# A fused linear-attention and gated state-space kernel: copies, scans and transposes in another order, and a flag read earlier

## The chip, the cores and the metric

The kernel runs on one core of one Trainium2 chip. The metric is device time in microseconds (us) of one launch. The core has five engines that run their own instruction streams and meet at semaphores: TensorE (PE in the profile, its weight loads PEld), VectorE (DVE), ScalarE (ACT), GpSimd (POOL) and SyncE (SP), which here only issues DMAs. Matmul results land in PSUM banks; everything else lies in SBUF.

## The reference, cut to what matters

Two blocks follow one another. The first is a recurrence per batch and head, the second a gated scan between two matrix products:

```python
# q, k, v, alpha: (4, 8, 768, 48)
for t in range(S):
    state = alpha[:, :, t, :, None] * state + np.einsum('bhd,bhe->bhde', k[:, :, t], v[:, :, t])
    y[:, :, t] = np.einsum('bhd,bhde->bhe', q[:, :, t], state)
x = y.transpose(0, 2, 1, 3).reshape(B, S, H * D)          # (4, 768, 384)

proj = x @ w_in                                           # 384 -> 2 * 512
val, gate = proj[..., :D_inner], proj[..., D_inner:]
a = np.exp(A_log)
for t in range(S):
    h = a[0, 0] * h + val[:, t, :]
    ys[:, t, :] = h
silu = gate * (1.0 / (1.0 + np.exp(-gate)))
return silu * ys @ w_out                                  # 512 -> 384
```

## The kernel before

**Tiling.** The 4 x 768 steps are cut into 12 blocks of 256 steps, three to a batch. A block of the attention is worked in chunks of 64 steps: the decays are folded into the operands as running products (tile `P`, a scan forward over `al`, the turned alphas; tile `V`, a scan backward), so that inside a chunk everything is matmuls. Zq is q times `P`, Zk is k times `V`. Raw q, k and alpha come from DRAM in rows and are turned on VectorE with `turn` (line 600, one instruction of 128x1024 elements each).

**One turn.** The main loop runs over `n` from 0 to 11; its turns overlap three blocks. In turn `n` the kernel projects block `n` with `w_in` (four calls of `project`, 12 matmul records each on line 988, 48 in all), does values, states and the carried part of the attention of block `m = n + 1` (`second` and `third`: lines 834, 866, 847), and prepares block `n + 2`: its alphas were turned at the end of the turn before, its k and q are turned and scaled during the turn, its scores (line 798) and masks come at the end. `project(n, cc)` also has a scan `hh` on VectorE (line 995) that reads its PSUM bank, a Silu on ScalarE (`sg`, line 1006) and a product `f_last` on GpSimd (line 1008). Because only four PSUM banks are handed round for such products (the string `taken` fixes which), `project(n, 3)` writes the bank that the scan of `project(n, 1)` has read.

**Order by hand.** The schedule is manual: each engine runs its instructions as the Python program emits them, and only semaphores make it wait. The preparation of a block is a generator, `products(l)`, with a `yield` behind each step: turn alpha, turn k, scan P, scan V, Zk, turn q, Zq. `go(count)` advances it, so where `go` stands decides where these VectorE instructions lie among the scans `hh`.

**Output.** For turns 2 to 10 the product with `w_out` is done in seven half-size products instead of eight (`output_parts(n)`, line 1064 for the matmuls and 1072 for the PSUM copies on ScalarE). It is a generator too. `pa` is a product whose copy goes to `s1` (profile name `wide`), `pd` one whose copy goes to `s7` (profile name `wide_S`, the copy to a tile that no matmul reads), `pc` one whose copy goes to `s5` (`wr`). After its copy, the bank `pa` takes a second product on top, and so do `pd` (records `mm<-wide_S,f_last`) and `pc`. TensorE runs: `pa` (4 records), `pd` (4), `pc` (4), second `pa` (4), second `pd` (4), `pb` (4), second `pc` (4), 28 in all. The second product on a bank waits for the copy from it.

**y's way into xT.** `join(m, engines)` copies the two PSUM tiles of y to `yst` (lines 960, 961), moves pieces of it that change partitions by eight DMAs (line 963, four on SP, four on POOL), and returns `rest`, which copies the straight pieces, two of 48x256, directly from PSUM to `xT` on ScalarE (line 966).

**Turns that end differently.** Turns 1 and 3 (`late`) leave the scores and masks of the next block until behind their output products; turn 1 has a body of its own, turn 3 ends in the `else` branch, and so does turn 10, which has no further block to prepare. Turn 2 and turns 4 to 9 end in the branch with `masks(..., between=...)`: the first part of `output_parts` is emitted between the mask products, then `rest()`, then the next part.

**Flag.** The fast path checks that its inputs allow the folded decays. `check_flag` (end of turn 10) reduces the checks to one integer in SBUF, every engine reads it into a register (line 1342, at the end of turn 11) and branches at line 1366: to a general version, or to the last output product (line 1373). On the measured inputs the latter is taken.

Of the kernel before, what the change touches and what calls it, by code (L numbers as in the profile page):

```python
# [346 lines left out]
def fast(  # L347
# [22 lines left out]
    nc = tc.nc  # L370
# [6 lines left out]
    NG = S // GC  # L377
    N = B * NG
# [23 lines left out]
    def load_raw(name, m, engine):  # L402
        if m >= N:
            return
        b, g = divmod(m, NG)
        src = srcs[name]
        to = raws[name][:, 0:4 * ROW].rearrange("p (h x) -> p h x", h=4)
        for i in range(2):
            for odd in range(2):
                n = ROW - 16 - 16 * odd  # L410
                engine.dma_start(
                    out=to[ds(64 * i + 32 * odd, 32), :, 0:n],
                    in_=src[b, ds(4 * i, 4), ds(g * GC, GC), :]
                    .rearrange("h (c j) d -> c h (j d)", c=32)[:, :, ds(32 * odd, n)])
# [77 lines left out]
    flag = const.tile([1, 1], I32, name="flag")  # L492
# [194 lines left out]
    def bank(tag=None):  # L687
        if tag:
            return ps_at.tile([C, 512], FP32, tag=tag, name=tag)
        return ps_mm.tile([C, 512], FP32, tag=f"mm{next(taken)}", name="mm")  # L690
# [376 lines left out]
    def output_parts(n):  # L1067
        b, g = divmod(n, NG)
        (B11, B12), (B21, B22) = blocks
        T1, T2, T3 = sums_w  # L1070
        S1, S2, S3, S4, U2, s5 = (parts_f[x] for x in ("S1", "S2", "S3", "S4", "U2", "s5"))
        copy = lambda to, t: nc.scalar.activation(to, t, AF.Copy)
        pa, pd = [bank()[:, 0:HM] for _ in range(2)]
        product(pa, quarter(0, 0), B11, True)
        copy(s1, pa)
        product(pd, S3, T3, True)
        yield
        copy(s7, pd)
        pc = bank()[:, 0:HM]
        product(pc, S1, T1, True)  # L1080
        copy(s5, pc)
        product(pa, quarter(0, 1), B21, False)
        o_sb = [rows.tile([C, DM], FP32, tag="o_sb", name="o_sb") for _ in range(G)]
        copy(o_sb[0][:, 0:HM], pa)
        product(pd, quarter(1, 1), T4, False)
        pb = bank()[:, 0:HM]
        product(pb, S2, T2, True)
        product(pc, S4, B22, False)
        nc.gpsimd.tensor_add(s7, s7, s5)
        yield  # L1090
        nc.vector.tensor_add(U2, s1, pb)
        nc.vector.tensor_add(o_sb[1][:, 0:HM], U2, pd)
        nc.vector.tensor_add(o_sb[0][:, HM:], U2, pc)
        nc.gpsimd.tensor_add(o_sb[1][:, HM:], U2, s7)
        for c in range(G):
            nc.sync.dma_start(out=out[b, ds(g * GC + c * C, C), :], in_=o_sb[c])
        yield
# [28 lines left out]
    last = P[:, :, GC]  # L1126
# [63 lines left out]
    for n in range(N):  # L1190
# [37 lines left out]
        elif n == 1:  # L1228
            scores(m)
            masks(m)  # L1230
            h3, f3 = project(0, 3, True)
            f2()
            P = scan_P(3)
            h3()
            values(m, True)
            st = states(m)
            add_banks(m, st)
            for f in fs_late:
                f()
# [12 lines left out]
            load_v(4, nc.sync)  # L1252
            f1()
            junk(3)
            V = scan_V(3, P)
            f2 = project(n, 2)
            scaled_k(3, tk, V)
            f2()
            output(0)
            sum_weights()  # L1260
            f3 = project(n, 3)
            tq = plain("q")
            turn("q", tq)
            load_raw("q", 4, nc.sync)
            scaled_q(3, tq, P)
            f3()
            go(1)
        else:
            if n == 2:
                first(m)  # L1270
            if n - 1 not in late:
                go(1)
                if n == N - 2:
                    check_w(5)
                next(outs, None)
                second(m)
                go(1)
                if n == N - 2:
                    check_w(0)
            else:  # L1280
                go(2 if n == 2 else 1)
            f0 = project(n, 0)
            f0()
            if n == N - 2:
                check_w(1)
            if n == 2:
                go(1)
            load_raw("a", n + 3, nc.sync)
            load_raw("k", n + 3, nc.sync)
            go(1)  # L1290
            f1 = project(n, 1)
            f1()
            if n < N - 1:
                sum_early()
            if n - 1 in late:
                second(m)
            if n == 4:
                go(1)
            if n == N - 2:
                check_w(2)  # L1300
            go(1)
            f2 = project(n, 2)
            f2()
            if n == N - 2:
                check_end()
            go(1)
            load_raw("q", n + 3, nc.sync)
            f3 = project(n, 3)
            f3()
            if m + 1 < N:  # L1310
                go(1)
            if n == N - 3:
                check_w(3)
            if n < N - 1:
                sum_late()
            rest = third(m)
            if n < N - 1:
                outs = output_parts(n)
            if n not in late and m + 1 < N:
                scores(m + 1)  # L1320
                masks(m + 1, between=lambda: next(outs))
                if m >= NG:
                    rest()
                    add_up(m, (3,))
                next(outs)
                go(1)
                if n == N - 3:
                    check_w(4)
            else:
                if m < N and m >= NG:  # L1330
                    rest()
                    add_up(m, (3,))
                if n < N - 2:
                    go(1)
                    for _ in outs:
                        pass
            load_v(m + 2, nc.sync)
        if n == N - 2:
            check_flag()
        if n == N - 1:  # L1340
            tc.mark_branch_hint_location("last", hint=0, engines=[mybir.EngineType.PE, mybir.EngineType.Activation, mybir.EngineType.DVE, mybir.EngineType.SP, mybir.EngineType.Pool])
            value = nc.values_load(flag[0:1, 0:1], min_val=0, max_val=1)
        if n == 1:
            output(n)
        if n == N - 2:
# [66 lines left out]
```

## Time and profile before

| what | value |
|---|---|
| median of 3 runs | 273.99 us (273.46 to 274.56) |
| the profiled execution's own time | 274.39 us |
| span of the profile | 272.7 us, 9967 instructions |
| PE busy | 265.9 us, 97% of the span |
| DVE busy | 234.7 us, 86% |
| POOL busy | 161.6 us, 59% |
| ACT busy | 111.5 us, 41% |
| granted TensorE clock | 0.999 of full speed |

The profile is of one execution. A row of its timeline reads: start in us from the span's start, duration, engine, line of the kernel, operation, output<-inputs by the program's names, shapes, count of merged records, and in brackets the engine's idle time before it with what ended that time. Two things must be known to read it. A matmul record lasts longer than the distance to the next one, since matmuls are pipelined, so distances between starts say more than durations. And four records that begin on a waiting engine are listed with 0.92 us instead of 0.81, so a held group can be told by its duration.

### The profile page before, as it was taken

How to read it: one execution, taken by the hardware profiler on the slowest of the kernel's cores; microseconds unless marked ns; L12 is line 12 of the kernel's file. 1: busy time of each engine (PE TensorE's matmuls, PEld its weight loads, DVE VectorE, ACT ScalarE, POOL GpSimd, SP SyncE). 2: the span in 40 equal slices, each digit the busy share in tenths (PEclk: the TensorE clock that was granted, in tenths of full speed). 3: DMA queues.
4: the chain of work that ended last, by engine and by line, in shares of the span. 5: the costliest groups of instructions: out<-in, count | busy, mean ns of one | idle time of the engine just before them, and what ended most of it. 6: DMA issues, size and time to landing. Idle time of an engine off the chain costs nothing.

```text
span 272.7 us, 9967 instructions
## 1 busy us (share of the span) xinstructions
PE 265.9 (97%) x4168; PEld 230.3 (84%) x4168; DVE 234.7 (86%) x316; ACT 111.5 (41%) x270; POOL 161.6 (59%) x185
## 2 busy tenths in 40 slices
PE   8999999999998999999999999999999999999995
PEld 6988888877786888888988988988988889888874
DVE  6979998996899999699999998999998998882430
ACT  3767766462341631441542433524525515214111
POOL 8122323175116997689985995996876976646000
PEclk9999999999999999999999999999999999999999
DMA  6937984998692669396588479595587501201101
GB/s 185 308 123 239 295 188 154 241 194 208 195 219 72 139 158 226 94 232 160 113 213 174 103 193 196 118 242 143 138 206 158 139 2 31 75 0 46 60 7 58
DMA packets 52304, 41.19 MB, mean 151 GB/s; under 512 B 27392, under 2 KB 50944, under 8 KB 52256
## 3 DMA queue, kind: packets, MB, share of 16 engines
q1 hardware_dynamic: 49328, 37.34, 55.2%
q0 software_dynamic: 1536, 2.20, 3.0%
q10 hardware_dynamic: 1392, 0.99, 1.2%
q8 instruction: 34, 0.56, 0.9%
q14 instruction: 14, 0.11, 0.2%
HBM read 32.54 MB, written 4.72 MB: 137 GB/s over the span
## 4 chain that ended last, share of the span: by engine, by line
PE 82%; DVE 10%; issue 2%; ACT 2%; DMA 1%; POOL 1%; DVEq 0%; ACTq 0%; POOLq 0%
PE mm L988 42%; PE mm L1064 15%; PE y L834 4%; PE y L847 4%; PE mm L1022 4%; PE mm L798 3%; PE s L798 3%; PE s L866 3%; DVE P L635 2%; PE mm L1373 2%; DVE V L654 2%; PE mm L707 1%; DMA raw_a<-in_alpha_dram 1%; DVE hh L995 1%; DVE k L600 1%
## 5 line engine op out<-in xcount | busy, mean ns | idle before, releaser
L988 PE MATMUL mm<-xT,w_in 128*128 128x256 f32 x576 | 129.7, 382 | 0.8 <-DVE hh L995 0.7
L988 PEld LDWEIGHTS mm<-xT,w_in 128*128 128x128 f32 x576 | 107.8, 190 | 16.9 <-DVE hh L995 1.1
L1006 ACT ACTIVATE sg<-mm 128x256 f32<-128x256 f32 x48 | 18.4, 384 | 89.2 <-PE mm L988 84.2
L1008 POOL TENSOR_TENSOR f_last<-sg,hh 128x256 f32<-128x256 f32 x36 | 30.2, 845 | 30.6 <-ACT sg L1006 21.7
L886 POOL TENSOR_TENSOR sum<-sum,dS 128x192 f32<-128x192 f32 x30 | 38.3, 1276 | 3.7 <-ACT dS L874 2.3
L635 DVE TENSOR_TENSOR_SCAN P<-al,lower 128x1028 f32<-128x1028 f32 x12 | 30.1, 2510 | 0.3
L995 DVE TENSOR_TENSOR_SCAN hh<-a_dec,hh,mm 128x256 f32<-128x256 f32 x32 | 23.4, 730 | 8.0 <-PE mm L988 7.7
L654 DVE TENSOR_TENSOR_SCAN V<-al,ends 128x1028 f32<-128x1028 f32 x12 | 29.3, 2439 | 0.4
L963 POOL DMA_DIRECT2D xT<-yst x44 | 22.5, 516 | 4.6 <-ACT yst L960 3.2
L556 POOL TENSOR_TENSOR w_in<-w_in,wr 128x768 int32<-128x768 int32 x4 | 7.3, 1823 | 25.9 <-DVE wr L551 16.1
L1064 PE MATMUL mm<-wide,wr 128*128 128x192 f32 x108 | 20.5, 326 | 0.0
L600 DVE STREAM_TRANSPOSE k<-raw_k 128x1024 f32<-128x1024 f32 x9 | 18.4, 2049 | 0.0
L600 DVE STREAM_TRANSPOSE q<-raw_q 128x1024 f32<-128x1024 f32 x9 | 18.2, 2025 | 0.0
L1064 PEld LDWEIGHTS mm<-wide,wr 128*128 128x128 f32 x108 | 18.0, 190 | 0.0
L818 POOL TENSOR_TENSOR AK<-AK,mask 128x512 f32<-128x512 f32 x9 | 13.4, 1494 | 7.7 <-ACT AK L814 7.6
L874 ACT ACTIVATE dS<-s 128x384 f32<-128x384 f32 (+1 forms) x18 | 7.4, 461 | 23.8 <-PE s L866 23.8
L619 DVE TENSOR_TENSOR Zk<-k,V 128x1024 f32<-128x1024 f32 (+1 forms) x14 | 16.5, 1181 | 0.1
L600 DVE STREAM_TRANSPOSE al<-raw_a 128x1024 f32<-128x1024 f32 x8 | 16.4, 2051 | 0.0
L1064 PE MATMUL mm<-w_out,f_last 128*128 128x192 f32 x72 | 15.8, 342 | 0.1
L610 DVE TENSOR_TENSOR Zq<-q,P 128x1024 f32<-128x1024 f32 (+1 forms) x14 | 15.2, 1087 | 0.0
L847 PEld LDWEIGHTS y<-Zq,sum 48*64 48x64 f32 x656 | 11.7, 134 | 3.9 <-issue 2.5
L834 PEld LDWEIGHTS y<-AK,v 64*64 64x64 f32 x352 | 12.1, 134 | 2.9 <-issue 2.9
(188 smaller groups left out, 503.4 us busy)
## 6 DMA issues: line engine op xcount, KB each, us to landing
v<-in_v_dram SPq DMA_DIRECT2D x22, 192.0 KB, 3.3
out_dram<-o_sb SPq DMA_DIRECT2D x22, 192.0 KB, 2.7
raw_k<-in_k_dram SPq DMA_DIRECT2D x18, 184.0 KB, 4.7
raw_q<-in_q_dram SPq DMA_DIRECT2D x18, 184.0 KB, 4.3
raw_k<-in_k_dram SPq DMA_DIRECT2D x18, 176.0 KB, 5.0
raw_q<-in_q_dram SPq DMA_DIRECT2D x18, 176.0 KB, 4.7
wbits<-in_moe_w_in_dram SPq DMA_DIRECT2D x8, 384.0 KB, 5.4
raw_a<-in_alpha_dram SPq DMA_DIRECT2D x16, 184.0 KB, 3.9
```

Of the source, the lines that this page charges most:

```text
L600: nc.vector.transpose(out=by_runs(to).rearrange("p h c j -> p h j c"), in_=raws[name][:, 0:4 * ROW].rearrange("p (h j d) -> p h j d", h=4, ...
L635: nc.vector.tensor_tensor_scan(out=P, data0=al[:, 0:4 * GP], data1=lower.rearrange("p h t -> p (h t)"), initial=0.0, op0=ALU.mult, op1=ALU ...
L654: nc.vector.tensor_tensor_scan(out=V[:, ::-1], data0=al[:, 1:4 * GP + 1][:, ::-1], data1=ends.rearrange("p h t -> p (h t)")[:, ::-1], init ...
L834: nc.tensor.matmul(ys[m][i][ds(64 * s, 64), e, ds(c * C + h * L, L)], v_sb[rows, c, 4 * i + p, :], As[i][rows, c, p, :], start=across and ...
L847: nc.tensor.matmul(ys[m][i][ds(64 * s, 64), e, ds(u * L, L)], Ss[j][rows, p, :], Zqs[m % 2][rows, u, p, D:], start=False, stop=True, skip_ ...
L886: nc.gpsimd.tensor_add(Ss[j][:, :, 0:D], Ss[j - 1][:, :, 0:D], part)
L963: engines[n % len(engines)].dma_start(out=xT[to, a], in_=st[rows, i, e])
L988: nc.tensor.matmul((pv, pg)[vg], w_ins[cc][:, kk, vg, :], xT[:, kk, :], start=(kk == 0), stop=(kk == NK - 1))
L995: nc.vector.tensor_tensor_scan(out=hh, data0=a_dec[:, cc:cc + 1].to_broadcast([C, GC]), data1=pv, initial=prev_h[cc][:, GC - 1:GC] if n % ...
L1006: nc.scalar.activation(sg, pg, AF.Silu)
L1008: f = lambda: engine.tensor_mul(fs[n][cc], sg, hh)
L1064: nc.tensor.matmul(o, a[:, k], b[k] if type(b) is list else b[:, k], start=start and k == 0, stop=k == KC - 1, skip_group_check=True)
```

## The change

No instruction is added or taken away; all edits move instructions in the order of an engine.

1. In `output_parts`, a `yield` is added behind the copy of `s7`. At the ends of turns 2 and 4 to 9, `next(outs)` is called once more ahead of `rest()`, so that the copy `s7` goes ahead of y's two straight copies. At the ends of turns 3 and 10, `next(outs)` is called twice ahead of `rest()`, so that both copies, `s1` and `s7`, go ahead of them. In turn 10 the tiny matmul of `check_flag` (line 587) comes to stand behind the first 8 of the 28 records as a consequence.
2. In turn 2, the scan `hh` of `project(2, 1)` goes ahead of the product Zk of block 4 (one `go(1)` moves from ahead of `project(2, 1)` to behind `f1()`).
3. At the end of turn 1, block 4's k is turned right behind its alphas (`go(2)` for `go(1)`), ahead of the two mask products `A` of block 3 on VectorE, and turn 2 has one `go` fewer.
4. In turn 11, the flag is read into registers ahead of `project(11, 3)` instead of behind it.

```diff
@@ output_parts
         product(pd, S3, T3, True)
         yield
         copy(s7, pd)
+        yield
         pc = bank()[:, 0:HM]
         product(pc, S1, T1, True)
         copy(s5, pc)
@@ end of turn 1
             scaled_q(3, tq, P)
             f3()
-            go(1)
+            go(2)
@@ turns 2 and on
             else:
-                go(2 if n == 2 else 1)
+                go(1)
             f0 = project(n, 0)
...
             load_raw("k", n + 3, nc.sync)
-            go(1)
+            if n != 2:
+                go(1)
             f1 = project(n, 1)
             f1()
...
-            if n == 4:
+            if n in (2, 4):
                 go(1)
...
             load_raw("q", n + 3, nc.sync)
+            if n == N - 1:
+                tc.mark_branch_hint_location("last", hint=0, engines=[...])
+                value = nc.values_load(flag[0:1, 0:1], min_val=0, max_val=1)
             f3 = project(n, 3)
             f3()
...
                 masks(m + 1, between=lambda: next(outs))
-                if m >= NG:
-                    rest()
-                    add_up(m, (3,))
+                next(outs)
+                rest()
+                add_up(m, (3,))
                 next(outs)
                 go(1)
...
             else:
-                if m < N and m >= NG:
+                if m < N:
+                    next(outs)
+                    next(outs)
                     rest()
                     add_up(m, (3,))
...
-        if n == N - 1:
-            tc.mark_branch_hint_location("last", hint=0, engines=[...])
-            value = nc.values_load(flag[0:1, 0:1], min_val=0, max_val=1)
```

More of the change, by code (lines that the diff above doesn't have):

```diff
@@ L1307, in fast @@
             load_raw("q", n + 3, nc.sync)
+            if n == N - 1:
+                tc.mark_branch_hint_location("last", hint=0, engines=[mybir.EngineType.PE, mybir.EngineType.Activation, mybir.EngineType.DVE, mybir.EngineType.SP, mybir.EngineType.Pool])
+                value = nc.values_load(flag[0:1, 0:1], min_val=0, max_val=1)
             f3 = project(n, 3)
@@ L1339, in fast @@
             check_flag()
-        if n == N - 1:
-            tc.mark_branch_hint_location("last", hint=0, engines=[mybir.EngineType.PE, mybir.EngineType.Activation, mybir.EngineType.DVE, mybir.EngineType.SP, mybir.EngineType.Pool])
-            value = nc.values_load(flag[0:1, 0:1], min_val=0, max_val=1)
         if n == 1:
```

## The prediction

> **What bounds the kernel now.** I read the busy time by stretches first, then TensorE's own rows wherever one group starts later than its predecessor's pace would have it, then the engine that released it.
>
> ```profile
> 131.00:264.00 133.00, 132.56 (x1942) 117.91 (x1941) 114.85 (x149) 48.25 (x127) 92.38 (x105) 1.00 0.50 120
> ```
>
> The columns behind the length are PE, PEld, DVE, ACT and POOL. PE is busy 132.56 of 133.00 us, at full granted clock: half of the kernel is TensorE alone, and an edit on another engine is worth only what it takes out of PE's row of starts. Busy time hides small holds, because a record lasts longer than its distance to the next one. So I go by starts. References first, from the chain of waits and from turn 10:
>
> ```profile
> 122.07 5.38 PE mm L988 x24
> 148.22 0.47 PE y L847 x32
> ...
> 251.00 0.81 PE L1064 MATMUL mm<-wide_S,f_last 128*128 128x192 f32 x4
> 251.65 0.81 PE L1064 MATMUL mm<-wide,wr 128*128 128x192 f32 x4
> ```
>
> Unheld, 24 projection records take 5.38 us (2.69 for 12), 32 carried records 0.47, four output records 0.65 (251.65 - 251.00) with a listed duration of 0.81. Now PE in turn 2:
>
> ```profile
> 80.16 2.86 PE L988 MATMUL mm<-xT,w_in 128*128 128x256 f32 x12
> 83.67 2.86 PE L988 MATMUL mm<-xT,w_in 128*128 128x256 f32 x12 [0.65 <-DVE hh L995]
> 86.46 0.46 PE L847 MATMUL y<-Zq,sum 48*64 48x64 f32 x16
> 87.20 0.41 PE L847 MATMUL y<-Zq,sum 48*64 48x64 f32 x16
> 87.85 0.46 PE L847 MATMUL y<-Zq,sum 48*64 48x64 f32 x16 [0.23 <-POOL sum L886]
> 88.13 0.95 PE L798 MATMUL s<-Zq,Zk 48*64 48x112 f32 x32
> 91.83 0.81 PE L1064 MATMUL mm<-w_out,f_last 128*128 128x192 f32 x4
> 92.89 0.92 PE L1064 MATMUL mm<-wide_S,f_last 128*128 128x192 f32 x4 [0.24 <-ACT wide_S L1072]
> ```
>
> Three holds. The projections take 86.46 - 80.16 = 6.30 instead of 5.38: 0.92 lost on the scan `hh`. The last 32 carried records take 88.13 - 87.20 = 0.93 instead of 0.47: 0.46 lost on GpSimd's `sum`. The second `pd` comes 92.89 - 91.83 = 1.06 behind the second `pa` instead of 0.65, 0.41 late, and starts slowly, 0.92 instead of 0.81: 0.52 lost on the copy `s7`. Together 1.90.
>
> ```profile
> 109.25 1.46 PE L1064 MATMUL mm<-wide,wr 128*128 128x192 f32 x8
> 110.80 0.92 PE L1064 MATMUL mm<-w_out,f_last 128*128 128x192 f32 x4
> 131.23 1.46 PE L1064 MATMUL mm<-wide,wr 128*128 128x192 f32 x8
> 132.53 0.81 PE L1064 MATMUL mm<-w_out,f_last 128*128 128x192 f32 x4
> 133.25 0.92 PE L1064 MATMUL mm<-wide_S,f_last 128*128 128x192 f32 x4
> ...
> 232.35 0.92 PE L1064 MATMUL mm<-wide_S,f_last 128*128 128x192 f32 x4
> 248.81 1.46 PE L1064 MATMUL mm<-wide,wr 128*128 128x192 f32 x8
> 250.25 0.92 PE L1064 MATMUL mm<-w_out,f_last 128*128 128x192 f32 x4
> ```
>
> Eight records at pace take 132.53 - 131.23 = 1.30. In turn 3 the second `pa` starts 1.55 behind, 0.25 late, plus 0.11 of slow start: 0.36. In turn 10 it is 1.44, 0.14 late, plus 0.11: 0.25. In turns 4 to 9 (first at 133.25, last at 232.35, six) the second `pd` starts 0.72 behind the second `pa` instead of 0.65, plus 0.11: 0.18 each. No wait list shows these six; the 0.92 does. Nothing else behind 92 us is held, apart from the branch at the end. All holds that the change can reach: 1.90 + 0.36 + 6 x 0.18 + 0.25 = 3.59 us.
>
> **Edit 1, the copies.** What the second `pd` waits for, in turn 4:
>
> ```profile
> 132.08 0.76 ACT L966 ACTIVATE xT<-y 48x256 f32<-48x256 f32 x2
> 132.87 0.33 ACT L1072 ACTIVATE wide_S<-mm 128x192 f32<-128x192 f32 x1
> ```
>
> The copy ends at 133.20, PE starts at 133.25. With the order changed it takes the place at 132.08. Its own input, the first `pd`, is the first half of the group at 131.23, whose fourth record starts 3 x 0.16 later at 131.72; with the 0.33 that one record lasts (0.81 less three steps of 0.16) it is done at 132.05. So the copy ends near 132.41, 0.77 ahead of the 133.18 at which PE would come unheld. The hold goes: 6 x 0.18 = 1.08. The two straight copies move 0.33 back and end near 133.17; ahead of the next projection, which reads xT, PE still has the 12 records from 133.18 on, 3 x 0.65 = 1.95 us, and `s5`, next on ScalarE, keeps its place. No DMA and no queue is passed, and none is issued by the moved copies. Without that cover, a straight copy that came last would cost at most its own 0.33 a turn. Bounds: 0 to 1.08; I take 1.08.
>
> In turns 3 and 10 both `s1` and `s7` (0.33 each) pass the straight copies (0.76), so PE's second `pa`, 0.25 and 0.14 late, is covered: 0.36 and 0.25. In turn 10 xT is wanted at once, as turn 11 projects right behind the 28 records. The pieces moved by DMA are not touched. The first `pd` is done at 248.81 + 0.49 + 0.33 = 249.63, `s7` at 249.96, the straight copies 0.76 later at 250.7, and PE ends the 28 records at 251.65 + 2 x 0.65 - 0.25 = 252.7: 2 us to spare. I take 0.61 for both turns, and 0.5 as lower bound, since the flag's matmul now stands among the 28 and may start slowly once more (0.11).
>
> **Edits 2 and 3, VectorE in turn 2.** VectorE's rows, and GpSimd's beside them:
>
> ```profile
> 69.81 2.02 DVE L600 STREAM_TRANSPOSE al<-raw_a 128x1024 f32<-128x1024 f32 x1
> 72.79 0.42 DVE L813 TENSOR_TENSOR A<-s,mask 128x256 f32<-128x256 f32 x1 [0.96 <-PE s L798]
> 73.56 0.42 DVE L813 TENSOR_TENSOR A<-mm,mask 128x256 f32<-128x256 f32 x1 [0.34 <-PE mm L798]
> 73.90 2.05 DVE L600 STREAM_TRANSPOSE k<-raw_k 128x1024 f32<-128x1024 f32 x1
> 75.80 2.23 DVE L635 TENSOR_TENSOR_SCAN P<-al,lower 128x1028 f32<-128x1028 f32 x1
> 81.73 1.23 DVE L619 TENSOR_TENSOR Zk<-k,V 128x1024 f32<-128x1024 f32 x1
> 82.87 0.74 DVE L995 TENSOR_TENSOR_SCAN hh<-a_dec,hh,mm 128x256 f32<-128x256 f32 x1
> 85.99 1.35 DVE L610 TENSOR_TENSOR Zq<-q,P 128x1024 f32<-128x1024 f32 x1
> ...
> 74.22 1.28 POOL L818 TENSOR_TENSOR AK<-AK,mask 128x512 f32<-128x512 f32 x1 [5.75 <-ACT AK L814]
> 85.66 2.13 POOL L886 TENSOR_TENSOR sum<-sum,dS 128x192 f32<-128x192 f32 x2
> ```
>
> `hh` ahead of Zk saves it 82.87 - 81.73 = 1.14: it would end at 83.61 - 1.14 = 82.47, and PE wants the bank at 80.16 + 2.69 = 82.85. The 0.92 goes even if VectorE gains nothing else. Zk comes later by one scan, 0.7 us; the scores want it at 88.13, or at 86.75 if all comes.
>
> The k transpose would start behind al, at 71.7, and fill the 0.96 + 0.34 us in which VectorE waits for scores. Its rows of k were asked for early:
>
> ```profile
> 61.63 1.96 SPq L411 DMA_DIRECT2D raw_k<-in_k_dram  x4
> ...
> DMA to landing us min/median/max: 3.0/4.3/5.3
> ```
>
> Issued by 63.59, landed by 68.9 at the latest: 2.8 us to spare. The load of the next k goes out behind it and stays behind alpha's four DMAs on SP. Two transposes at 75.80 - 73.90 = 1.90 put the first `A` at 69.81 + 3.80 = 73.61 and, at 0.34 each, P at 74.29, 1.51 us earlier. The later `A` are no loss: the values that read them stand behind 24 projection records, at 73.5 + 5.38 = 78.9 or so, and the PSUM bank of the second `A` behind 12. But where P would start GpSimd's AK product runs, from 74.22 to 75.50. How these two meet is shown elsewhere:
>
> ```profile
> 93.21 3.27 DVE L635 TENSOR_TENSOR_SCAN P<-al,lower 128x1028 f32<-128x1028 f32 x1
> ...
> 116.08 3.18 POOL L818 TENSOR_TENSOR AK<-AK,mask 128x512 f32<-128x512 f32 x1 [1.86 <-ACT AK L814]
> ```
>
> P takes 2.23 alone but 3.27 where GpSimd was already at work; the AK product takes 1.28 alone but 3.18 where P had just begun. The one that starts second waits. [...]
>
> By the starts above AK leads by 0.07 us, so I take P as second: it ends at 75.50 + 2.23 = 77.73 instead of 78.03. VectorE's chain gains 0.30. Then the sums: GpSimd's second sum ends at 85.66 + 2.13 = 87.79, 0.45 behind the end of Zq at 87.34, since Zq held it. Zq's end moves to 87.04, the sum's to 87.49, and PE gains 0.30 there, not 0.92 + 0.46 = 1.38. The 0.52 of `s7` comes on top, because that copy, 0.41 late, now passes 0.76 us of copies. So turn 2 gives 0.82. If P is first, Zq ends at 85.83 and the sum at 86.28, ahead of PE, which would want it at 87.85 - 1.38 = 86.47, and all 1.90 comes. Bounds: 0.52, if VectorE gains nothing, to 1.90. In turn 3 PE would then be 0.4 us or so earlier than VectorE is; whether the scans there keep pace I leave to the third rival.
>
> **Edit 4, the flag.** Register loads and branches, by line, and the chain of waits at the end:
>
> ```profile
> L1342 PEldq TENSOR_LOAD <-flag x1: 486/486/486, 259.4 to 259.4; - x1
> ...
> L1366 PEldq COMPARE_BRANCH  x1: 3708/3708/3708, 260.0 to 260.0; - x1
> ...
> 263.47 0.44 issue
> ```
>
> PE's sequencer read the flag at 259.4, 4 us ahead of the array's last projection at 263.47; then the branch sat 3.71 us until the array was through. So the load was hidden before and is hidden in its new place, under the same 4 us of queued matmuls; the pause of 0.44 belongs to the branch. Edit 4 gives 0. Bounds: a gain of 0.44 at most, a loss of 0.49 if the array ran dry at the load. [...]
>
> **Sum.** 0.82 + 0.36 + 1.08 + 0.25 = 2.51 us. The profiled execution, 274.39 with a span of 272.7, would become 271.9 with 270.2. It lies 0.40 above the median of the runs shown, 273.99, which becomes 271.5.
>
> **Rivals.**
> - P first (all holds go): 3.59, 270.4 us. For it: the lead of AK is only 0.05 us. Against: a scan that arrives second loses 1.1 us, as at 93.21.
> - The six regular turns give nothing, because the copy `s7` in its new place waits for its mask neighbours or another input of the second `pd` comes last: 2.51 - 1.08 = 1.43, 272.6 us. Against it: the 0.77 us to spare.
> - The change doesn't do what it says: PE's holds only move on, turn 3's scans and sums giving back what turn 2 gains, and the copies show no more than in turn 10: 0.3 to 0.6, about 273.6 us. For it: VectorE's 0.30 in turn 2 is thin.
> - Slower: TensorE, now with hardly a pause, is granted less clock. Place: everything behind 92 us, some 170 us of PE work. Price: 1.7 us for each hundredth of clock; it decides from a granted clock of 0.985 on (2.51 / 170), and at 0.97 the time is 273.99 - 2.51 + 5.1 = 276.6 us. Against it: the stretch from 131 us is already 99.7% busy at 1.00.
>
> **How the numbers follow.** Chances: forecast 0.47, P first 0.24, regular turns without gain 0.13, nothing of note 0.10, slower 0.06. The range goes from 270.2, just below P first with all holds gone, to 272.8, which takes in the third case and VectorE's lower bound (2.51 - 0.30 = 2.21, 271.8) with the flag's loss of 0.49. What a measurement here can tell from no change is about 0.5%, 1.37 us, so faster means below 272.62: the first two cases and 0.08 of the third, which lies on the line, 0.79; within 0.5%: 0.15; slower: 0.06.
>
> **What would show it.** Right: in turns 4 to 9 the second `pd` 0.65 behind the second `pa`, listed with 0.81; the 28 records at 4.75 us; in turn 2 no wait of line 988 for `hh`; P near 74.3 with 3.2 to 3.4 us, or AK with over 3; a `sum` still waited for by PE; the pause of 0.44 ahead of the last product unchanged. Wrong: records of 0.92 at `wide_S`, a new wait of PE in turn 3, a gap in PE's row ahead of `project(11, 3)`, or a granted clock below 0.99.

## The result, and the profile after

| | before | changed |
|---|---|---|
| median | 274.07 us (273.46 to 274.56, 6 runs) | 270.52 us (6 runs; 269.78 to 271.40 in five of them) |
| the profiled execution's own time | 274.39 us | 269.92 us |
| span of the profile | 272.7 us | 268.2 us |
| granted TensorE clock | 0.999 | 1.00 |

The ratio is 0.9868, with a 95% interval of 0.9843 to 0.9893: 3.6 us faster, 2.9 to 4.3. A sixth execution of the changed kernel, 274.46 us at a granted clock of 0.992, counts in its median only, not in the range, the ratio and the interval; the 17 others on record were granted 0.998 to 1.00.

First TensorE and its neighbours, rows picked from the timeline of the changed kernel (start, duration, engine, line, operation, output<-inputs, shapes, count):

```profile
71.29 1.00 PE L798 MATMUL s<-Zq,Zk 48*64 48x112 f32 x32
...
73.77 3.36 POOL L818 TENSOR_TENSOR AK<-AK,mask 128x512 f32<-128x512 f32 x1 [5.75 <-ACT AK L814]
73.77 2.28 DVE L635 TENSOR_TENSOR_SCAN P<-al,lower 128x1028 f32<-128x1028 f32 x1
...
79.71 5.45 PE L988 MATMUL mm<-xT,w_in 128*128 128x256 f32 x24
85.08 0.46 PE L847 MATMUL y<-Zq,sum 48*64 48x64 f32 x16
...
85.83 0.65 PE L847 MATMUL y<-Zq,sum 48*64 48x64 f32 x32
86.30 0.95 PE L798 MATMUL s<-Zq,Zk 48*64 48x112 f32 x32
...
87.95 0.92 PE L1064 MATMUL mm<-w_out,f_last 128*128 128x192 f32 x4
...
129.38 0.35 ACT L1072 ACTIVATE wide_S<-mm 128x192 f32<-128x192 f32 x1
129.60 0.76 ACT L966 ACTIVATE xT<-y 48x256 f32<-48x256 f32 x2
129.83 0.81 PE L1064 MATMUL mm<-w_out,f_last 128*128 128x192 f32 x4
130.48 0.81 PE L1064 MATMUL mm<-wide_S,f_last 128*128 128x192 f32 x4
...
244.95 0.81 PE L1064 MATMUL mm<-wide,wr 128*128 128x192 f32 x4
245.69 0.19 PE L587 MATMUL s<-one,okc 128*1 128x1 f32 x2
245.81 0.92 PE L1064 MATMUL mm<-wide,wr 128*128 128x192 f32 x4
246.57 0.81 PE L1064 MATMUL mm<-w_out,f_last 128*128 128x192 f32 x4
```

Read it as the prediction was read, by distances of starts. In turn 2 the projections take 85.08 - 79.71 = 5.37 us where they took 6.30, and the last 32 carried records 86.30 - 85.83 = 0.47 where they took 0.93. In turn 4 the second `pd` stands 130.48 - 129.83 = 0.65 behind the second `pa`, with 0.81 listed and not 0.92, and so it does in turn 2. The copy `wide_S` at 129.38 now runs ahead of the two straight copies. All three holds of turn 2 are gone, and P was not second: the scan took 2.28 us, and it is GpSimd's AK product that was held, with 3.36 us where it takes 1.28 alone. A listed 0.92 by itself does not tell a hold: the first four of the 28 output records, at 87.95 behind records of another shape, have it without a wait.

Turn 10 is not as forecast: the flag's matmul (L587) stands among the output records, and the group behind it starts slowly, 246.57 - 245.81 = 0.76 to the next group instead of 0.65.

The chain of waits of the changed kernel at its end (start, duration, engine, tile, line, count):

```profile
226.07 4.75 PE mm L1064 x28
...
249.33 10.36 PE mm L988 x48
259.69 5.19 PE mm L1377 x24
```

And the same rows of the kernel before:

```profile
229.65 4.92 PE mm L1064 x28
...
253.12 10.36 PE mm L988 x48
263.47 0.44 issue
263.91 5.43 PE mm L1373 x24
```

In turn 9 the 28 output records take 4.75 instead of 4.92, the last product follows the projections at once (249.33 + 10.36 = 259.69) where 0.44 lay between, and that product itself is 0.24 shorter. The chain counts ends. By starts, the last 48 projection records lead the last product by 10.96 us before and by 10.36 after, so its 0.44 and 0.24 are a pause of 0.60 and 0.07 in the last product.

Where the 4.47 us between the two profiled executions (274.39 - 269.92) went (gains from the unrounded starts):

| place | before | after | gained | forecast |
|---|---|---|---|---|
| turn 2, projections | 6.30 | 5.37 | 0.92 | together 0.82 |
| turn 2, carried records | 0.93 | 0.47 | 0.46 | |
| turn 2, 28 output records | 5.26 | 4.75 | 0.51 | |
| turn 3, 28 output records | 5.10 | 4.75 | 0.36 | 0.36 |
| turns 4 to 9, 28 records each | 4.92 | 4.75 | 6 x 0.175 = 1.05 | 1.08 |
| turn 10, with the flag's matmul | 5.01 | 4.97 | 0.04 | 0.25 |
| last projections to last product | 10.96 | 10.36 | 0.60 | 0 |

That is 3.94 us, with 0.07 in the last product 4.01. The other 0.46 was there ahead of every edit that can reach it: the scores of turn 1 start at 71.29 here and at 71.75 in the kernel before. In the twelve other profiles, with the same instructions up to there, they start at 71.13 to 73.24, so this part is spread between executions. So three terms of the forecast's 2.51 us were missed, turn 2, turn 10 and the end, and the questions for the chip were three: do the holds go straight into the time; is P always first; and what is the pause at the end?

### The profile page after: what moved, and what is told of

Its sections match the earlier page's. It is cut to its first block, busy times and chain, and to the rows that moved or that the text cites. A ratio compares the mean times of both kernels' runs of the same rounds, so it can differ in the third digit from the quotient of the medians.

```text
span 268.2 us, 9966 instructions
## 1 busy us (share of the span) xinstructions
PE 263.3 (98%) x4168; PEld 230.4 (86%) x4168; DVE 233.8 (87%) x316; ACT 111.6 (42%) x270; POOL 165.9 (62%) x185
## 4 chain that ended last, share of the span: by engine, by line
PE 91%; DVE 2%; DMA 2%; issue 1%; ACT 1%; POOL 1%; SPq 0%; DVEq 0%; POOLq 0%
PE mm L988 47%; PE mm L1064 16%; PE y L834 4%; PE y L847 4%; PE mm L1022 4%; PE s L798 4%; PE mm L798 3%; PE s L866 3%; DMA raw_q<-in_q_dram 2%; PE mm L1377 2%; PE mm L707 1%; PE mm L702 1%; PE mm L703 1%; DVE P L635 1%; POOL w_in L556 1%
## 5 line engine op out<-in xcount | busy, mean ns | idle before, releaser
L1008 POOL TENSOR_TENSOR f_last<-sg,hh 128x256 f32<-128x256 f32 x36 | 31.2, 874 | 24.2 <-ACT sg L1006 19.6
L886 POOL TENSOR_TENSOR sum<-sum,dS 128x192 f32<-128x192 f32 x30 | 37.5, 1251 | 3.0 <-ACT dS L874 1.4
L654 DVE TENSOR_TENSOR_SCAN V<-al,ends 128x1028 f32<-128x1028 f32 x12 | 28.7, 2391 | 0.4
L818 POOL TENSOR_TENSOR AK<-AK,mask 128x512 f32<-128x512 f32 x9 | 15.6, 1729 | 7.7 <-ACT AK L814 7.6
```

The source lines that it names most:

```text
L654: nc.vector.tensor_tensor_scan(out=V[:, ::-1], data0=al[:, 1:4 * GP + 1][:, ::-1], data1=ends.rearrange("p h t -> p (h t)")[:, ::-1], init ...
L886: nc.gpsimd.tensor_add(Ss[j][:, :, 0:D], Ss[j - 1][:, :, 0:D], part)
L1008: f = lambda: engine.tensor_mul(fs[n][cc], sg, hh)
```

## The experiments

The expectations use these names. Theory H: each hold taken away goes into the time; rival G: PE's holds only move on. Rival S: with P second, behind the AK product, a hold stays at the sums. Theory F supposes that the branch sends for its instructions when it starts, and that whatever stands ahead of it on PE's sequencer takes from its lead; rival D: the branch waits until the array is through, as the prediction had it.

### One edit or pair at a time

Edit 1 alone, on the kernel before:

```diff
@@ output_parts
         copy(s7, pd)
+        yield
@@ ends of turns 2 and 4 to 9
+                next(outs)
                 rest()
@@ ends of turns 3 and 10
+                    next(outs)
+                    next(outs)
                     rest()
```

> The kernel before with edit 1 alone (the copies ahead of y's straight copies). Theory H (every hold on TensorE's row of starts goes straight into the time): the second pd of turns 4 to 9 is no longer held, 28 records 4.75 us instead of 4.92, six times 0.17 = 1.05; turn 3 5.10 to 4.75 = 0.36; turn 2 5.26 to 4.75 = 0.51; turn 10 at most 0.1, since the flag's matmul starts slowly among the 28; the hold on the scan hh (0.92) and on sum (0.46) in turn 2 stays. Sum 1.9 to 2.0 us, ratio 0.993. The pause ahead of the last product stays at 0.4 to 0.6. Rival G (holds move on): the 28 records stay near 4.9 or another group grows by as much, ratio 0.997 to 1.000.

Measured: 272.1 us median, ratio 0.9924 (0.9902 to 0.9947), so 2.1 us gained (1.5 to 2.7). The output records take 4.75 us in all turns from 2 to 9; the holds on `hh` (6.30) and on the sum (0.93) in turn 2 stand unchanged. Turn 10 takes 1.497 + 0.120 + 3.354 = 4.97, as in the changed kernel. The holds that went, 0.51 + 0.36 + 1.05 + 0.04 = 1.96, agree with the time.

Edits 2 and 3 alone:

```diff
@@ end of turn 1
-            go(1)
+            go(2)
@@ turn 2
-                go(2 if n == 2 else 1)
+                go(1)
...
-            go(1)
+            if n != 2:
+                go(1)
             f1 = project(n, 1)
...
-            if n == 4:
+            if n in (2, 4):
                 go(1)
```

> The kernel before with edits 2 and 3 alone (scan ahead of Zk, k behind alpha). [...] Ratio 0.995. Rival S (P second, as the prediction had it): P takes over 3 us, the carried records stay held, 0.3 to 0.9 us gained, ratio 0.997 to 0.999.

Measured: 272.96 us, ratio 0.9943 (0.9921 to 0.9966), 1.6 us gained (0.9 to 2.2), where theory H has 0.92 + 0.46 = 1.38. P came first (2.27, AK 3.37). PE in turn 2 of this kernel, from the timeline:

```profile
86.94 0.65 PE L847 MATMUL y<-Zq,sum 48*64 48x64 f32 x32
87.41 0.95 PE L798 MATMUL s<-Zq,Zk 48*64 48x112 f32 x32
...
91.11 0.81 PE L1064 MATMUL mm<-w_out,f_last 128*128 128x192 f32 x4
92.09 0.92 PE L1064 MATMUL mm<-wide_S,f_last 128*128 128x192 f32 x4 [0.17 <-ACT wide_S L1072]
```

The sum holds nothing any more (87.41 - 86.94 = 0.47), and the copy `s7` still holds the second `pd` (92.09 - 91.11 = 0.98, listed with 0.92). Its hold is 0.44 with the slow start, where it was 0.52, so edit 1 and this pair take away different holds and hardly touch each other's.

Edit 4 alone:

```diff
@@ turn 11
             load_raw("q", n + 3, nc.sync)
+            if n == N - 1:
+                tc.mark_branch_hint_location("last", hint=0, engines=[...])
+                value = nc.values_load(flag[0:1, 0:1], min_val=0, max_val=1)
             f3 = project(n, 3)
...
-        if n == N - 1:
-            tc.mark_branch_hint_location("last", hint=0, engines=[...])
-            value = nc.values_load(flag[0:1, 0:1], min_val=0, max_val=1)
```

> The kernel before with edit 4 alone (flag read ahead of the last projection). Theory F (TensorE's branch waits some 3.4 to 3.7 us for instructions that its own start sends for, and the load stands between the queued matmuls and the branch): the branch starts 0.5 to 0.6 earlier against the array's end, the pause of 0.44 goes, 48 projections and pause take 10.36 instead of 10.96 and the last product about 0.2 less: 0.6 to 0.8 us, ratio 0.997 to 0.998. Rival D (the prediction's: the branch waits until the array is through): the pause stays at 0.44, ratio 1.000.

Measured: 273.82 us, ratio 0.9976 (0.9960 to 0.9991), 0.7 us gained (0.2 to 1.1). No hold of the turns changes; the pause at the end, by starts, is 0.23 instead of 0.60. The three gains, 2.1 + 1.6 + 0.7 = 4.4, agree within their intervals with the 3.6 of the whole.

### The flag back at the end, and read twice

The changed kernel with edit 4 undone:

> The changed kernel with edit 4 undone (flag read behind the last projection). Theory F: the pause ahead of the last product comes back, 0.4 to 0.6 us in the 48 projections and 0.1 to 0.2 in the product: 0.6 to 0.8 us slower than the changed kernel, 2.8 to 3.0 faster than before, ratio 0.989 to 0.990. Rival D: as fast as the changed kernel, no difference at the end.

Measured: 271.19 us median (270.43 to 272.58), ratio 0.9874 (0.9849 to 0.9900). That is 0.7 above the changed kernel, with intervals that overlap, so the rows have to show the effect. The pause is back (10.95 from the last 48 projections to the last product, 0.59 over pace). And in its profiled execution, the slowest of its five, P was second:

```profile
74.99 1.27 POOL L818 TENSOR_TENSOR AK<-AK,mask 128x512 f32<-128x512 f32 x1 [5.44 <-ACT AK L814]
75.31 3.11 DVE L635 TENSOR_TENSOR_SCAN P<-al,lower 128x1028 f32<-128x1028 f32 x1
...
87.06 0.41 PE L847 MATMUL y<-Zq,sum 48*64 48x64 f32 x16
88.01 0.46 PE L847 MATMUL y<-Zq,sum 48*64 48x64 f32 x16 [0.54 <-POOL sum L886]
88.29 0.95 PE L798 MATMUL s<-Zq,Zk 48*64 48x112 f32 x32
```

VectorE was 0.32 us behind AK there, since its work in turn 1 had run late: it starts `al` 1.63 us ahead of TensorE's scores, and 1.93 ahead in the changed kernel. The 32 carried records take 88.29 - 87.06 = 1.23 instead of 0.47. That is the prediction's own case. Why VectorE was late in that execution wasn't settled.

Then, with the flag back at the end, a second read behind the first:

```diff
...
+            value = nc.values_load(flag[0:1, 0:1], min_val=0, max_val=1)
+            nc.values_load(flag[0:1, 0:1], min_val=0, max_val=1)
```

> The changed kernel with the flag read at the end of turn 11 as before the change, and read twice there. Theory F (the branch sends for its instructions when it starts, and what stands ahead of it on PE's sequencer takes from its lead): the branch starts about 0.5 to 0.6 us later than with one load, the 48 projection records up to the last product take 11.4 to 11.7 us instead of 10.95 (10.36 without a pause), so a pause of about 1.0 in place of 0.42. Rival D (the branch waits until the array is through, the prediction's reading): the second load is hidden like the first, the pause stays at 0.3 to 0.6.

Measured: 271.32 us in its one execution; 11.28 us from the last 48 projections to the last product, a pause of 0.92. The doubling itself did not take place where it was meant to: in the rows of that line only SP has a second load, and TensorE has a wait of 51 ns in its place. So this run doubles nothing on PE. It still adds to the rows of the branch. From the register loads and branches by line, first of the changed kernel with the flag back, read once at the end:

```profile
L1346 PEldq TENSOR_LOAD <-flag x1: 487/487/487, 257.7 to 257.7; - x1
L1370 PEldq COMPARE_BRANCH  x1: 3693/3693/3693, 258.2 to 258.2; - x1
```

of the changed kernel:

```profile
L1312 PEldq TENSOR_LOAD <-flag x1: 487/487/487, 253.1 to 253.1; - x1
L1370 PEldq COMPARE_BRANCH  x1: 3397/3397/3397, 255.7 to 255.7; - x1
L1370 ACTq COMPARE_BRANCH  x1: 76/76/76, 259.8 to 259.8; - x1
```

and of the changed kernel in a later run of it, its third run (listed below):

```profile
L1370 PEldq COMPARE_BRANCH  x1: 2098/2098/2098, 256.0 to 256.0; - x1
```

The chain of waits of that third run at its end:

```profile
249.66 10.36 PE mm L988 x48
260.02 5.19 PE mm L1377 x24
```

The branch is over at 256.0 + 2.1 = 258.1, while the projections run up to the last product without a gap (249.66 + 10.36 = 260.02; by starts it begins at 259.86). The array was busy for 1.76 us after the branch ended, so the branch does not wait for the array: rival D falls by these rows. The first profile of the changed kernel agrees: its branch ends at 259.06, 0.47 ahead of the last product.

What it may wait for stands in the DMA rows (queue and kind, packets, MB, share of 16 DMA engines' time in the stretch). Of the kernel before, in the stretch from 261.0 to 262.0 us; its branch runs from 260.0 to 263.7, and from 260.0 to 261.0 there is no packet:

```profile
q8 instruction: 1, 0.02, 7.9%
```

and of the third run, in the stretch from 255.3 to 256.0 us, ahead of its branch at 256.0; from 256.0 to 258.0 no packet starts:

```profile
q8 instruction: 1, 0.02, 11.8%
```

One packet of instructions of 16 KB takes 7.9% x 16 x 1.0 = 1.27 us in the one and 11.8% x 16 x 0.7 = 1.32 in the other. The traces also hold each packet's own start and duration. In 13 of the 14 profiles the packet starts 1.03 to 1.10 us into the branch, and the branch takes 3.4 to 3.9 us; in the one where it started 0.63 us ahead of the branch, 2.1. From the packet's end to the end of the branch it is 1.40 to 1.42 us in all 14. Eight of them:

| profile | load | lead of PE over the branch | packet | branch | pause |
|---|---|---|---|---|---|
| before | at the end | 3.27 | 1.27 | 3.71 | 0.60 |
| edit 1 alone | at the end | 3.27 | 1.13 | 3.61 | 0.51 |
| flag back | at the end | 3.27 | 1.22 | 3.69 | 0.59 |
| flag read twice | at the end | 3.12 | 1.42 | 3.87 | 0.92 |
| edit 4 alone | ahead | 3.86 | 1.47 | 3.93 | 0.23 |
| changed | ahead | 3.87 | 0.95 | 3.40 | 0 |
| changed, second run | ahead | 3.87 | 1.38 | 3.87 | 0.17 |
| changed, third run | ahead | 3.87 | 1.32, early | 2.10 | 0 |

The lead is the time from the start of the branch to where the last product would start at pace (10.36 behind the first of the 48 projections). The last product starts 0.17 us behind the end of the branch, or at pace, whichever is later: pause = branch + 0.17 - lead, or nothing. This gives the pause within 0.02 us in these eight profiles, and in the six others too (0.39, 0.70 and 0.63 with the load at the end; 0.01, 0 and 0 with it ahead). Moving the load, 0.49 us and the 0.10 between its end and the branch, out from between the projections and the branch adds 0.6 to the lead (3.86 to 3.87 against 3.27 to 3.28 with one load at the end). How much of it shows depends on how long the packet took, 0.95 to 1.47 us. That the branch waits for this packet is inferred from the constant 1.4 us; no run took the packet away, and why the packet came early in the third run stays open. Edit 4 also moves the line with the branch hint. The traces show no instruction of that line, and in 13 profiles the packet starts equally far into the branch wherever the line stands; but no run moved the load and the hint apart.

The packet of the third run began 0.63 us ahead of the branch, so that branch cannot have sent for it. That the branch sends for the packet in the other 13 profiles is the author's reading of its place, 1.03 to 1.10 us into the branch; no run shows what sends for it.

### P and the AK product

The changed kernel twice more, unaltered:

> The changed kernel once more, unaltered, to see which of the two ways P and the AK product meet in turn 2. Theory 'a race that goes either way': in the changed kernel's first profile P led (P 2.28 us, AK 3.36, 32 carried records 0.47), in the one with the flag read back AK led (P 3.11, AK 1.27, carried records 1.24), so either may show; if AK leads, the records of line 847 end 0.77 later and the span is 268.2 + 0.8 = about 269.0 us. Rival 'P always leads with the change as it stands': P 2.2 to 2.4 us and a span of 268.2 within 0.3. Median expected near 270.5 either way.

> The changed kernel a third time, as the measure for the others of this call. Theory 'the prediction was right in size by two errors': turn 2 gives 1.9 when P leads, 1.1 when AK leads, and the end gives 0.4 to 0.6 by the flag; median 270.3 to 270.9 us. No rival; the profile shows once more which of P and the AK product leads (carried records of line 847 at 0.47, or at 1.24).

Measured: 270.64 us (269.80 to 271.32) and 270.53 us (269.93 to 272.35); ratios 0.9855 (0.9821 to 0.9888) and 0.9882 (0.9850 to 0.9913). P led in both. The rows of the third run:

```profile
74.10 3.36 POOL L818 TENSOR_TENSOR AK<-AK,mask 128x512 f32<-128x512 f32 x1 [5.75 <-ACT AK L814]
...
74.11 2.27 DVE L635 TENSOR_TENSOR_SCAN P<-al,lower 128x1028 f32<-128x1028 f32 x1
```

AK is listed 0.01 us ahead and yet is the one that waits. So it was in all seven profiles in which AK led by 0.03 us or less (this, the two other profiles of the changed kernel, edits 2 and 3 alone, edit 3 alone, the flag read twice, the flag's matmul first): P took 2.27 to 2.28. Where AK led by 0.32, in the profile of the flag back, it went first. Why VectorE wins the near tie, and how far behind it still would, no run shows.

To force that order, four memsets of 128x64 ahead of P in turn 2:

```diff
+        if m == 4:
+            for _ in range(4):
+                nc.vector.memset(pad, 0.0)
```

> Four small memsets (128x64, not read by anything) are put on VectorE ahead of the scan P of turn 2, so that GpSimd's AK product always starts ahead of P. Nothing is left out of the computation. Theory 'P second costs its hold': P lists over 3 us, AK 1.3, the 32 carried records of line 847 take 0.47 + 0.7 to 1.0 and the time is 0.7 to 1.1 us above the changed kernel, about 271.4 us. Rival 'the hold moves on, because turn 3 has slack for it': the carried records are held likewise, but the 28 records of turn 2 or PE in turn 3 gain it back, and the time stays within 0.3 us of the changed kernel, 270.5. Rival 'the prediction's own price', that with P second the scan hh goes free and the sum holds 0.3 less than before: 1.07 us of the 3.59 is lost, 271.6.

```profile
74.57 1.27 POOL L822 TENSOR_TENSOR AK<-AK,mask 128x512 f32<-128x512 f32 x1 [5.75 <-ACT AK L818]
...
75.22 2.78 DVE L636 TENSOR_TENSOR_SCAN P<-al,lower 128x1028 f32<-128x1028 f32 x1
...
86.63 0.41 PE L851 MATMUL y<-Zq,sum 48*64 48x64 f32 x16
87.59 0.46 PE L851 MATMUL y<-Zq,sum 48*64 48x64 f32 x16 [0.55 <-POOL sum L890]
87.87 0.95 PE L802 MATMUL s<-Zq,Zk 48*64 48x112 f32 x32
```

These are rows of its timeline. AK went first, P lists 2.78 and ends at 78.00, near where the prediction put it, and the carried records take 87.87 - 86.63 = 1.24, 0.77 over pace. Its median is 271.54 us (271.25 to 271.67), 0.9 above the 270.64 of the changed kernel measured beside it: the hold is not given back later. P second costs less than the forecast charged for it: 0.77 of turn 2's 1.90 is lost, not 1.08.

To force the other order, a GpSimd copy of one element of the second masked A ahead of AK, and, as a second edit, the flag's matmul ahead of turn 10's output records:

```diff
+        if m == NG:
+            nc.gpsimd.tensor_copy(out=pad, in_=A0[0:1, G - 1, 3, 0:1])
@@ ends of turns 3 and 10
+                if n == N - 2:
+                    check_flag()
...
-        if n == N - 2:
-            check_flag()
```

> The changed kernel with two more edits: a GpSimd copy of one element of the second masked A ahead of the AK product of turn 2, so that AK waits for VectorE's second A and P is already issued; and the flag's matmul put ahead of turn 10's 28 output records again. Nothing is left out. Theory 'both are open ends of the change': P 2.2 to 2.4 us and AK over 3 in every profile, 24 projection records 5.38 and 32 carried 0.47 in turn 2; turn 10 0.119 + 4.75 to 4.85 instead of 4.97, a gain of 0.1 to 0.2; time 0.1 to 0.5 us below the changed kernel's median and a narrower spread. Rival 'the copy costs GpSimd its sum': AK comes so late that the sum of line 886 holds PE, the 32 carried records take over 0.6, and the time is the changed kernel's or above it. Rival 'the slow start of 0.11 is the flag's neighbour wherever it stands': turn 10 stays at 4.97 to 5.0.

Its timeline:

```profile
74.18 2.12 POOL L819 COPY pad<-A 1x1 f32<-1x1 f32 x1 [5.90 <-DVE A L814]
76.26 1.27 POOL L821 TENSOR_TENSOR AK<-AK,mask 128x512 f32<-128x512 f32 x1
77.50 0.72 POOL L1011 TENSOR_TENSOR f_last<-sg,hh 128x256 f32<-128x256 f32 x1
...
76.88 1.36 DVE L652 TENSOR_TENSOR ratio<-P,ends 128x4 f32<-128x4 f32 x1
```

A miss. P is first, but the copy of one element now takes 2.12 us, to 76.30, beside P, which runs from 74.05 to 76.32; AK runs behind it, and VectorE's small product `ratio` takes 1.36 us, to the end of `f_last` at 78.22, where it took 0.54 in the changed kernel. VectorE loses 0.8, the carried records take 0.93, and the median is 270.86 us, no better than the changed kernel's 270.64. The other edit did what was expected: turn 10 takes 0.120 + 4.654 = 4.77.

### The two edits of turn 2, apart

Edit 2 alone, on the kernel before:

```diff
-            go(1)
+            if n != 2:
+                go(1)
             f1 = project(n, 1)
...
-            if n == 4:
+            if n in (2, 4):
                 go(1)
```

> Edit 2 alone on the kernel before: hh of project(2, 1) ahead of Zk. Theory 'the holds go straight into time, each edit by its own': the 24 projection records of turn 2 take 5.38 instead of 6.30, but Zk, Zq and the sum are no earlier, so the hold on the sum takes 0.46 + 0.92 less what Zk gains = about 1.0 to 1.4 in turn 2's carried records (they take 1.4 to 1.8 instead of 0.93): the gain is 0 to 0.3 us, span 272.4 to 272.7. Rival 'each edit is worth its own hold': the 32 carried records stay at 0.93, gain 0.92, span 271.8. Rival 'edit 2 does nothing, hh is late in any case': 24 records stay above 6.0.

and edit 3 alone:

```diff
@@ end of turn 1
-            go(1)
+            go(2)
@@ turn 2
-                go(2 if n == 2 else 1)
+                go(1)
```

> Edit 3 alone on the kernel before: k of block 4 turned right behind its alphas, the scan hh left behind Zk. Theory 'what turn 2 gains is what VectorE is earlier': P starts 1.5 us earlier, hh ends near 82.1 and is no longer waited for (24 projection records 5.38), and with P first the sum is free as well (32 carried records 0.47 to 0.6): gain 1.2 to 1.4 us, about 273.0 us; with P second the 24 records take 5.4 to 5.9 and the carried records 1.0 to 1.3, gain 0.4 to 0.8. Rival 'both edits are needed': hh still holds PE 0.5 us or more with P first, gain under 0.6 us.

From the timeline of edit 2 alone, turn 2:

```profile
87.78 0.41 PE L847 MATMUL y<-Zq,sum 48*64 48x64 f32 x16
89.15 0.46 PE L847 MATMUL y<-Zq,sum 48*64 48x64 f32 x16 [0.95 <-POOL sum L886]
89.43 0.76 PE L798 MATMUL s<-Zq,Zk 48*64 48x112 f32 x24
```

Edit 2 alone: 274.12 us, ratio 0.9988 (0.9967 to 1.0009), nothing that can be told from no change. The 24 projection records are free, 5.38 us, but the carried records take 89.43 - 87.78 = 1.65: of the 0.92 won at `hh`, 0.72 comes back as a longer wait for the sum. This is rival G, and for this edit it is what happens. Edit 3 alone: 272.91 us, ratio 0.9951 (0.9931 to 0.9971), 1.3 us gained, with P first, 5.38 for the 24 records and 86.68 - 86.11 = 0.57 for the carried ones. So what turn 2 gains is what VectorE is earlier. With P first, edit 2 is worth the 0.10 between 0.57 and 0.47.

### A version with the flag's matmul first

The changed kernel with `check_flag` ahead of turn 10's output parts (the second edit of the run that put P first), nothing else:

> The changed kernel with one more edit: check_flag is called ahead of turn 10's output parts, so that its matmul on line 587 stands ahead of the 28 records and not behind the first 8 of them. Theory 'the slow start is that of the group behind the flag's matmul': 0.12 + 4.65 instead of 4.97 us, so 0.2 us less than the changed kernel of this call, near 270.3 us, which its spread may hide. Rival 'the flag made earlier costs ScalarE or VectorE the copies in turn 10': 28 records above 4.75 us there, time as the changed kernel or above.

```profile
244.03 0.19 PE L587 MATMUL s<-one,okc 128*1 128x1 f32 x2
244.15 0.92 PE L1064 MATMUL mm<-w_out,f_last 128*128 128x192 f32 x4
...
248.81 1.46 PE L988 MATMUL mm<-xT,w_in 128*128 128x256 f32 x6
```

In this timeline turn 10 takes 248.81 - 244.03 = 4.78 us, 0.2 less than in the changed kernel. The median is 270.13 us (269.60 to 270.57), the lowest of all kernels here, with a ratio of 0.9858 (0.9834 to 0.9883). The interval overlaps that of the changed kernel measured beside it (0.9850 to 0.9913), so of the 0.4 us only the 0.2 in the row is shown.

## Why the prediction was right, and where it was not

The measured median lies 1.0 below the forecast of 271.5 us, inside the range, and the kernel became faster as forecast. That it is inside the range is owed to its lower end, which was set by the rival with P first: two steps of the forecast itself failed, as the list shows. Its order of reading, TensorE's starts first, found all holds of the turns and their sizes. Of the signs it named, the 0.65 with 0.81, the 4.75, no wait for `hh` and an AK over 3 came; a `sum` still waited for and an unchanged pause did not. The steps, one by one:

- **Edit 1, turns 2 to 9: right.** 1.05 us measured in turns 4 to 9 against 1.08, 0.36 in turn 3 as forecast, 0.51 in turn 2 against 0.52. The straight copies that come later held nobody.
- **Edit 1, turn 10: mis-sized.** 0.25 was taken and 0.04 came. The hold did go: 5.01 to the 4.77 of the kernel with the flag's matmul first is the 0.24. But the flag's matmul among the 28 costs 4.97 - 4.77 = 0.20. The prediction named this neighbour and priced it at 0.11, the slow start behind it; the last record ahead of it also loses 0.09 (245.69 - 244.95 = 0.74 for four records instead of 0.65).
- **Edits 2 and 3: the mechanism right, the order wrong.** "By the starts above AK leads by 0.07 us, so I take P as second" is the step that failed. The starts were added up from listed durations, 1.90 for a transpose and 0.34 for an `A`, and the steps measured were 1.87, 1.89 and 0.33, 0.32. That is 0.07 in all: the lead was as large as the error of its sum, and near ties within 0.03 us went to VectorE. The rival "P first" had turn 2 right with 1.90. Both orders occur: P led in all three profiles of the changed kernel, AK in the one with the flag back. With P second 1.13 comes (1.90 - 0.77) instead of 0.82, because P ended 0.37 and not 0.30 earlier than before, measured from the scores of turn 1 (78.00 - 72.09 against 78.03 - 71.75), and Zq was also shorter there, 1.18 instead of 1.35. The 1.1 us that the prediction read at 93.21 as the loss of a scan that arrives second holds two GpSimd instructions: that scan ends 2.16 us behind the end of the `sum` that follows AK (93.73 + 0.59 = 94.32).
- **Edits 2 and 3 as one chain: right.** The bound of 0.52, "if VectorE gains nothing", means that `hh` going free gives nothing by itself, because the sum waits for VectorE; the run of edit 2 alone shows that.
- **Edit 4: wrong.** "then the branch sat 3.71 us until the array was through. So the load was hidden" is the step that failed. The branch sat that long for itself, about 1.0 us, the instruction packet (1.27 us) and 1.4 us more, against a lead of 3.3 us. It was late by 0.4 to 0.9 in the profiles with the load at the end, and the load ahead of it on PE's sequencer, 0.49 with 0.10 behind it, was part of that. The bound named, a gain of 0.44, is what the chain lists as pause; by starts it is 0.60, and 0.37 to 0.60 of it was gained. The same branch took 76 ns on ScalarE, and on TensorE 3397 to 3930 ns in the 13 profiles in which the packet starts behind the start of the branch.
- **The sum.** 2.51 was too small by 1.07 (turn 2) and 0.60 (the end), and too large by 0.21 (turn 10) and 0.03 (turns 4 to 9): 3.94 of holds in the profiled pair. The medians give 3.55 or, by the ratio, 3.6; an execution with P second (0.77) or a long packet (0.17) would account for part of the rest, but the executions without a profile do not show it. That the rival's 3.59 comes so near to 3.55 is partly luck: it lacked the 0.60 at the end and had 0.21 too much at turn 10.
- **The other rivals.** The regular turns gave their gain. That holds only move on is true of edit 2 by itself and of nothing else. The clock was 1.00 in the changed kernel's profile.

## What to carry to other kernels

When a forecast hangs on which of two instructions starts first, and the lead is no larger than the rounding of the durations it was summed from, price both orders and forecast between them, or force the order and measure it. The scan moved out of the way of TensorE by edit 2 alone gained nothing (ratio 0.9988), since the next wait hung on the same engine's chain and 0.72 of the 0.92 us came back there; count what the engine as a whole is earlier. And look at what stands ahead of a branch on the sequencer: here the branch was late by 0.4 to 0.9 us, so the register load ahead of it, 0.49 us with 0.10 behind it, was on the critical path, with 3.3 us of matmuls still to run when the branch began.

## What the runs showed of the hardware

- TensorE's compare-and-branch took 3.4 to 3.9 us in the 13 profiles in which an instruction packet of 16 KB began 1.03 to 1.10 us after it, and 2.1 us in the one in which that packet had begun 0.63 us ahead of it; in all 14 it ended 1.40 to 1.42 us behind the packet's end. On ScalarE the same branch took 76 ns.
- Of the scan P on VectorE and the product AK on GpSimd, listed up to 0.03 us ahead of it, the scan ran first in seven profiles of seven (2.27 to 2.28 us, AK 3.36 to 3.38); with a lead of 0.32 or 0.65 the product did (1.27 us, P 3.11 and 2.78).
- A GpSimd copy of a single element, started 0.13 us behind P (74.05), took 2.12 us, to 0.02 us ahead of P's end. VectorE's product `ratio` of 128x4 elements, started at 76.88 in that run while GpSimd worked, took 1.36 us, to 78.24, through the end of that GpSimd instruction (77.53) and of the next one (78.22); it took 0.54 in the changed kernel. The scan at 93.21 in the kernel before, 3.27 us, also runs past the ends of two GpSimd instructions (93.77 and 94.32).
- The flag's matmul (128x1) among the output records (f32) cost 0.20 us beside its own 0.12: 0.09 at the group ahead of it and 0.11 at the group behind.
